# Gated linear attention with a gated feed-forward on one Trainium2 core: the first unit's two large products in full 32-bit type, weights split into parts behind them, and another order of the first transfers

## The chip, the cores and the metric

The kernel runs on one core of one Trainium2 chip. The metric is the device time of one execution in microseconds (us). A core has five engines with a queue each, worked off in order: TensorE (PE in the profile, its weight loads PEld), VectorE (DVE), ScalarE (ACT), GpSimd (POOL) and SyncE (SP), which here issues every transfer.

## The reference

For each of 4 batches and 8 heads a state of 48 x 48 runs over 768 positions; its output is the input of a feed-forward with a convolution of three taps as its gate.

```python
f = 1.0 / (1.0 + np.exp(-f_logit))
for t in range(S):
    state = f[:, :, t, :, None] * state + np.einsum('bhd,bhe->bhde', k[:, :, t], v[:, :, t])
    y[:, :, t] = np.einsum('bhd,bhde->bhe', q[:, :, t], state)
...
h = np.maximum(x @ w_in, 0.0)
for k in range(K):
    conv_out += conv_w[k][None, None, :] * hp[:, k:k + S, :]
gate = 1.0 / (1.0 + np.exp(-conv_out))
return (h * gate @ w_out).astype(np.float32)
```

x is y with its heads side by side (768 x 384 per batch), w_in is 384 x 1024, w_out 1024 x 384, and hp is h with a row of zeros on each side. The three weight tensors come as 64-bit floats.

## The kernel before

**Chunks.** The sequence is cut into chunks of 128 positions, six per batch, 24 in all, numbered n. For each chunk SyncE loads the gates' inputs (fb), k (kp), q (qp) and v. ScalarE takes exp and log of the gates (lines 167 and 168), TensorE sums them along the chunk with a triangular matrix (pl, line 193), and ScalarE raises the sums again (fi and fd, lines 197 and 198), by which k and q are multiplied (lines 210 and 211, on VectorE and GpSimd). TensorE transposes both (ptk, ptq, line 233) and ScalarE copies them out (kT, qT, line 235). Then come the scores (pa, line 281), VectorE's masked copy of them (am, line 283), the state's products and update (pk, lines 295 to 306) and the values (py, lines 318 and 321). For chunks 0 to 8 the cumulative sum is one product in full 32-bit type (tri32 and fb); later ones use two of type float32r, a reduced 32-bit type.

**Units.** Three chunks, half a batch, make a unit of the feed-forward, eight in all. The values are copied to xT twice: a high part in float32r by ScalarE (line 329) and what is left, the low part, by VectorE (line 330). Behind a unit's third chunk six transfers bring pieces of xT to other partitions (line 335). The first matrix product (mm1, line 358) makes eight blocks ph of 128 x 384; each takes three inner tiles, and for each of them three float32r products: high weight with high value, high weight with low value, low weight with high value. Behind each block come ScalarE's relu (hb, line 361) and first tap (line 363), VectorE's other taps (lines 369 and 370), ScalarE's tanh (line 372) and VectorE's closing multiplication (line 373); these are the gate steps, all in the tile g. The second product (mm2) goes by output tiles of 128 positions: g is split into high (gh, line 388, ScalarE) and low (gl, line 389, VectorE), and eight inner tiles with three float32r products each (line 395) make po, which ScalarE copies to ob and SyncE stores (lines 398 and 399). A unit with the first half of a batch owns two output tiles, the other one four.

**Weights.** Their 64-bit words are turned into two float32r parts by split_f64 (lines 90 to 107), piece by piece: w_in in six pieces of 128 x 512 (three inner tiles kt, two halves i of the 1024 columns), w_out in eight of 128 x 384. Per piece GpSimd clamps the upper words (line 98) and takes their sign (line 99), ScalarE scales the upper (line 100) and converts the lower words (line 101), VectorE merges them in two steps (lines 102 and 104), ScalarE casts the sum to the high part (line 106) and VectorE subtracts for the low one (line 107).

**What sets the order.** Everything is planned as small pieces with a number (lines 410 to 449), sorted by it, and written out; the numbers come from the table CFG and count in chunks. A scheduler then orders the instructions of each engine from there, so that the table moves them without fixing each place. From chunk 8 on the products of a chunk's values, state and scores are kept together (visit, lines 256 to 272). Raw weights, the tiles g and xT share slots: the raw halves of w_in and the first of w_out lie in the two slots of g, the other raw half of w_out in one of the three slots of xT.

## Time and profile before

| what | before |
|---|---|
| median of 3 runs (lowest to highest) | 373.13 us (373.02 to 373.95) |
| the profiled execution's own time | 373.25 us |
| its span, first to last instruction | 371.5 us |
| mean granted clock of TensorE | 0.97 of full speed |
| TensorE busy | 342.6 us, 92% |
| VectorE busy | 279.9 us, 75% |
| ScalarE busy | 239.4 us, 64% |
| GpSimd busy | 75.1 us, 20% |

Times in the profile run from the span's start; between its span and its own time lie 1.75 us. A row of the groups names line, engine, operation, output and inputs, shapes and count, then busy time, mean ns of one, and the idle time of the engine in front of it with what ended it. A row of a timeline names start, length, engine, line, operation and count, and in brackets the idle time in front of it. A full 32-bit product appears as two records. A row of stages names its bounds, its length, and for each engine busy time and count, then the granted clock, the DMA engines' busy share and GB/s. The chain of waits follows the work that ended last back to the start, with the time that each step adds to it.

### The profile page before, as it was taken

Reading aid. Unit: us, or ns where it says so; the run is one execution under the profiler, and the core shown is the slowest. Engines: PE = TensorE matmul, PEld = TensorE weight load, DVE = VectorE, ACT = ScalarE, POOL = GpSimd, SP = SyncE. Lnnn points to the kernel's source line nnn. Section 1 sums busy time; section 2 is a strip of 40 time slices with the busy share of each in tenths; the row PEclk is TensorE's granted clock in tenths of the full one; section 3 lists DMA queues with packets and bytes.
Section 4 is the critical chain, followed back from the end, with each engine's and each line's share of the span. In section 5 each row is a group of like instructions: output and inputs, shape, how many; then the busy total and the mean of one; then the engine's idle time right before and its main releaser. Section 6 shows DMA issues by size and latency. Waiting matters only on the chain.

```text
span 371.5 us, 7272 instructions
## 1 busy us (share of the span) xinstructions
PE 342.6 (92%) x2747; PEld 315.4 (85%) x2747; DVE 279.9 (75%) x407; ACT 239.4 (64%) x426; POOL 75.1 (20%) x103
## 2 busy tenths in 40 slices
...
GB/s 234 374 334 350 79 112 158 128 30 114 133 28 80 110 193 23 76 108 160 54 42 85 72 136 44 73 116 52 23 43 35 23 0 55 33 11 44 21 45 50
DMA packets 28853, 36.04 MB, mean 97 GB/s; under 512 B 10847, under 2 KB 20106, under 8 KB 28810
## 3 DMA queue, kind: packets, MB, share of 16 engines
...
## 4 chain that ended last, share of the span: by engine, by line
PE 59%; ACT 14%; DVE 11%; DMA 8%; issue 4%; SPq 1%; ACTq 0%; DVEq 0%
PE po L395 21%; PE ph L358 21%; PE py L321 5%; DMA wis<-in_moe_w_in_dram 4%; PE pa L281 4%; PE py L318 3%; DMA fb<-in_f_logit_dram 3%; DVE g L369 2%; PE pl L193 2%; DVE kp L210 2%; PE ptq L233 2%; ACT fb L167 2%; ACT g L363 1%; ACT fb L168 1%; DVE g L370 1%
## 5 line engine op out<-in xcount | busy, mean ns | idle before, releaser
L358 PE MATMUL ph<-xT,wi 128*128 128x384 f32 x576 | 112.6, 345 | 4.6 <-ACT ob L398 2.6
L358 PEld LDWEIGHTS ph<-xT,wi 128*128 128x128 f32 x576 | 101.1, 189 | 8.4 <-ACT ob L398 3.9
L395 PE MATMUL po<-wo,gh 128*128 128x384 f32 x384 | 99.4, 340 | 0.0
L395 PEld LDWEIGHTS po<-wo,gh 128*128 128x128 f32 x384 | 69.7, 188 | 0.1
L395 PE MATMUL po<-wo,gl 128*128 128x384 f32 x192 | 65.8, 343 | 0.0
L369 DVE SCALAR_TENSOR_TENSOR g<-hb,cw,g 128x384 f32<-128x384 f32 (+1 forms) x64 | 44.7, 701 | 14.6 <-ACT g L363 14.1
L372 ACT ACTIVATE g<-g 128x768 f32<-128x768 f32 (+1 forms) x32 | 27.1, 846 | 43.0 <-DVE g L370 42.9
L361 ACT ACTIVATE hb<-ph 128x384 f32<-128x384 f32 x64 | 31.2, 490 | 25.5 <-PE ph L358 25.4
L370 DVE SCALAR_TENSOR_TENSOR g<-hb,cw,g 128x384 f32<-128x384 f32 (+1 forms) x64 | 42.7, 666 | 3.4 <-DVE g L369 0.5
L373 DVE SCALAR_TENSOR_TENSOR g<-g,hb 128x768 f32<-128x768 f32 (+1 forms) x32 | 30.8, 964 | 16.7 <-ACT g L372 16.6
L389 DVE TENSOR_TENSOR gl<-g,gh 128x1024 fp32r<-128x1024 f32 (+4 forms) x34 | 32.1, 957 | 14.6 <-ACT gh L388 14.6
L363 ACT ACTIVATE g<-hb,cw 128x384 f32<-128x384 f32 (+1 forms) x64 | 39.3, 618 | 1.9
L211 POOL TENSOR_TENSOR qp<-qp,fd 128x384 f32<-128x384 f32 x22 | 28.8, 1307 | 53.3 <-ACT fd L198 43.3
L388 ACT CAST gh<-g 128x1024 fp32r<-128x1024 f32 (+4 forms) x34 | 26.4, 800 | 19.9 <-PE po L395 17.4
L395 PEld LDWEIGHTS po<-wo,gl 128*128 128x128 f32 x192 | 36.1, 188 | 0.9 <-issue 0.2
L321 PE MATMUL py<-am,v 128*48 128x128 f32 x384 | 28.9, 295 | 5.8 <-DVE am L283 5.8
L283 DVE COPY_PREDICATED am<-mask,pa 128x1024 f32<-128x1024 uint8 x24 | 31.6, 1316 | 1.8 <-PE pa L281 1.6
L281 PE MATMUL pa<-qT,kT 48*128 48x128 f32 x384 | 28.4, 285 | 3.5 <-ACT qT L235 3.5
L321 PEld LDWEIGHTS py<-am,v 128*48 128x48 f32 x384 | 21.9, 131 | 10.9 <-DVE am L283 6.8
L281 PEld LDWEIGHTS pa<-qT,kT 48*128 48x128 f32 x384 | 23.6, 187 | 8.2 <-ACT qT L235 4.9
L210 DVE TENSOR_TENSOR kp<-kp,fi 128x384 f32<-128x384 f32 x22 | 22.0, 1000 | 10.5 <-ACT fi L197 9.8
L318 PE MATMUL py<-qT,st 128*112 128x128 f32 x168 | 22.8, 279 | 0.0
...
## 6 DMA issues: line engine op xcount, KB each, us to landing
kp<-in_k_dram SPq DMA_DIRECT2D x24, 256.0 KB
qp<-in_q_dram SPq DMA_DIRECT2D x24, 256.0 KB
fb<-in_f_logit_dram SPq DMA_DIRECT2D x24, 192.0 KB
v<-in_v_dram SPq DMA_DIRECT2D x24, 192.0 KB
out_dram<-ob SPq DMA_DIRECT2D x24, 192.0 KB
wis<-in_moe_w_in_dram SPq DMA_DIRECT2D x6, 512.0 KB
...
```

What stands on the lines that cost most here:

```text
L281: nc.tensor.matmul(pa[:, j, p, :], kT[r, p, :], qT[r, p, :], start=True, stop=True)
L283: ready.setdefault(n, []).append(nc.vector.copy_predicated(am, mask, pa).ins)
L318: nc.tensor.matmul(py[:HP + D, p, :], s_b[n % 2][:, p, :], qT[:, p, :], start=(p == 0), stop=False)
L321: nc.tensor.matmul(py[HP * j:HP * j + D, p, :], vt[:, 2 * p + j, :], am[:, j, p, :], start=not inter and p == 0, stop=(p == NP - 1))
L358: nc.tensor.matmul(ph, wi[:, t, wl, f * P:(f + 1) * P], xts[b, hf][:, t, xl, :], start=(i == 0), stop=(i == 3 * KT - 1))
L361: nc.scalar.activation(hb[:, 2:HS + 2], ph, AF.Relu, scale=0.5)
L363: nc.scalar.activation(cv, hb[:, 1:n + 1], AF.Copy, scale=cw[:, 1, f:f + 1])
L369: nc.vector.scalar_tensor_tensor(cv, hb[:, 2:n + 2], cw[:, 2, f:f + 1], cv, ALU.mult, ALU.add)
L370: nc.vector.scalar_tensor_tensor(cv, hb[:, 0:n], cw[:, 0, f:f + 1], cv, ALU.mult, ALU.add)
L373: nc.vector.scalar_tensor_tensor(cv, cv, 1.0, h_b[:, fp:fp + 2, 1:n + 1], ALU.add, ALU.mult)
L389: nc.vector.tensor_tensor(lo, g[:, f:f + k], hi.bitcast(F32), ALU.subtract)
L395: nc.tensor.matmul(po, g[:, f, :], wo[:, f, wl, :], start=(i == 0), stop=(i == 3 * NF - 1))
```

## The change

**Types.** The function single replaces split_f64: it makes one 32-bit tile per weight piece out of the same words with the same two steps each on GpSimd, ScalarE and VectorE. The function split makes the high and low part out of that tile, with ScalarE's cast and VectorE's subtraction, and is planned by itself. For the first unit (u = 0, batch 0, first half) mm1 takes the 32-bit pieces and one product per inner tile, in full 32-bit type; so do the two output tiles that it owns, with g itself as the weight loaded, so that gh and gl are not made for them. The values of its three chunks are copied to xT once, in 32 bits, with no low part, and the transfers inside xT carry that half only. All other units compute as before.

**Tiles.** The high parts are wih and woh. The 32-bit pieces and the low parts share slots: seven for w_in's pieces, eight for w_out's. So a low part takes over the slot of an earlier 32-bit piece, once the first unit's products and the split have read it. The constant zeros for the products that keep TensorE warm at the start (wz) now lie in wih, where a high part is written later.

**Order.** In the table, the first nine chunks' gates are loaded 0.7 of a chunk earlier; w_in is loaded at -0.9 and 0.2 instead of -2.3 and -1.1 and converted from 2.6 and 3.3 on, instead of -0.7 and 0.9; w_out is loaded at 2.9 and 2.7 instead of 1.3 and 1.0 and converted from 4.0 on instead of 2.1; w_in is split from 4.6 and 6.0 on, w_out from 8.9 on; and the output tiles of each unit lie 0.9 instead of 1.2 thirds (or quarters) of a unit apart.

```diff
+    wl = ctx.enter_context(tc.tile_pool(name="wl", bufs=1))
...
     ft_all = const.tile([P, B, NC, NP], F32, name="ft_all")
-    wz = const.tile([P, WC], F32R, name="wz")
+    wih = const.tile([P, KT, DFF], F32R, name="wih")
+    woh = const.tile([P, NF, DM], F32R, name="woh")
+    wz = wih[:, KT - 1, DFF - WC:]
     nc.gpsimd.memset(wz.bitcast(F32), 0.0)
-    wi = const.tile([P, KT, 2, DFF], F32R, name="wi")
-    wo = const.tile([P, NF, 2, DM], F32R, name="wo")
+    w32, wlo = {}, {}
     cw = const.tile([P, 3, NF], F32, name="cw")
-    def split_f64(raw, n, hi, lo, nm):
+    def single(raw, n, w, nm):
         pr = raw.rearrange("p (n w) -> p n w", w=2)
         lw, hw = pr[:, :, 0], pr[:, :, 1]
...
         ms = wk.tile([P, 2, WC], I32, tag="gl", name=f"ms{nm}")
         m, s = ms[:r, 0, :n], ms[:r, 1, :n]
         hf, mf, sf = hw.bitcast(F32), m.bitcast(F32), s.bitcast(F32)
-        nc.gpsimd.tensor_scalar(hf, hf, F64_TOP, -F64_TOP, ALU.min, ALU.max)
-        nc.gpsimd.tensor_scalar(sf, hf, 0.0, 1.0, ALU.mult, ALU.mult)
-        nc.scalar.activation(mf, hf, AF.Copy, scale=2.0 ** -112)
+        nc.gpsimd.tensor_scalar(mf, hf, F64_TOP, -F64_TOP, ALU.min, ALU.max)
+        nc.gpsimd.tensor_scalar(sf, mf, 0.0, 1.0, ALU.mult, ALU.mult)
+        nc.scalar.activation(mf, mf, AF.Copy, scale=2.0 ** -112)
         nc.scalar.activation(lw, lw.bitcast(U32), AF.Copy, scale=2.0 ** -29)
         nc.vector.scalar_tensor_tensor(m, m, 3, s, ALU.logical_shift_left, ALU.bitwise_or)
-        w = hi.bitcast(I32) if lo is None else s
-        nc.vector.tensor_tensor(w, m, lw, ALU.add)
-        if lo is not None:
-            nc.scalar.copy(hi, mf)
-            nc.vector.tensor_tensor(lo, sf, hi.bitcast(F32), ALU.subtract)
+        nc.vector.tensor_tensor(w.bitcast(I32), m, lw, ALU.add)
+
+    def split(key, hi, name, **slot):
+        wlo[key] = wl.tile(list(hi.shape), F32R, name=name, **slot)
+        nc.scalar.copy(hi, w32[key])
+        nc.vector.tensor_tensor(wlo[key], w32[key], hi.bitcast(F32), ALU.subtract)
...
     def load_w_in(kt, i):
         nc.sync.dma_start(raw_in(kt, i), w_in[kt * P:(kt + 1) * P, i * WC:(i + 1) * WC].bitcast(I32))
+    def single_w_in(kt, i):
+        w32["i", kt, i] = wl.tile([P, WC], F32, tag="wi", name=f"wi{kt}_{i}", bufs=KT * DFF // WC + 1)
+        single(raw_in(kt, i), WC, w32["i", kt, i], f"wi{kt}_{i}")
+
     def split_w_in(kt, i):
-        cs = slice(i * WC, (i + 1) * WC)
-        split_f64(raw_in(kt, i), WC, wi[:, kt, 0, cs], wi[:, kt, 1, cs], f"wi{kt}_{i}")
+        split(("i", kt, i), wih[:, kt, i * WC:(i + 1) * WC], f"wil{kt}_{i}", tag="wi", bufs=KT * DFF // WC + 1)
     def load_w_out(f):
         nc.sync.dma_start(raw_out(f), w_out[f * P:(f + 1) * P, :].bitcast(I32))
+    def single_w_out(f):
+        w32["o", f] = wl.tile([P, DM], F32, tag="wo", name=f"wo{f}", bufs=NF)
+        single(raw_out(f), DM, w32["o", f], f"wo{f}")
+
     def split_w_out(f):
-        split_f64(raw_out(f), DM, wo[:, f, 0, :], wo[:, f, 1, :], f"wo{f}")
+        if f == 0:
+            split(("o", f), woh[:, f], f"wol{f}", tag="wi", bufs=KT * DFF // WC + 1)
+        else:
+            split(("o", f), woh[:, f], f"wol{f}", tag="wo", bufs=NF)
...
         xT = xts[b, hf]
         ts = slice((c % CPH) * P, (c % CPH + 1) * P)
         for r in [slice(0, HP + D)] if c > 0 or n == 0 else [slice(0, D), slice(HP, HP + D)]:
+            if (b, hf) == (0, 0):
+                nc.scalar.copy(xT[r, :, 0, ts].bitcast(F32), py[r])
+                continue
             nc.scalar.copy(xT[r, :, 0, ts], py[r])
             nc.vector.tensor_tensor(xT[r, :, 1, ts], py[r], xT[r, :, 0, ts].bitcast(F32), ALU.subtract)
         if c % CPH == CPH - 1:
             for t in range(KT):
                 for j in range(2):
                     s0, d0 = HP * j + GAP * t, HP * j + D
-                    nc.sync.dma_start(xT[d0:d0 + GAP, t, :, :].bitcast(F32), xT[s0:s0 + GAP, KT, :, :].bitcast(F32))
-
-    def moe(xts, wk, ps):
+                    m = 1 if (b, hf) == (0, 0) else 2
+                    nc.sync.dma_start(xT[d0:d0 + GAP, t, :m, :].bitcast(F32), xT[s0:s0 + GAP, KT, :m, :].bitcast(F32))
+
+    def moe(xts, wk, ps, whole):
         gts = {}
         def mm1(u, fp):
...
             for f in (fp, fp + 1):
                 hb = h_b[:, f]
                 ph = ps.tile([P, HS], F32, tag="mm", name=f"ph{u}_{f}", bufs=2)
-                i = 0
-                for t in range(KT):
-                    for wl, xl in ((0, 0), (0, 1), (1, 0)):
-                        nc.tensor.matmul(ph, wi[:, t, wl, f * P:(f + 1) * P], xts[b, hf][:, t, xl, :],
-                                         start=(i == 0), stop=(i == 3 * KT - 1))
-                        i += 1
+                fs = slice(f * P, (f + 1) * P)
+                i, cs = f * P // WC, slice(f * P % WC, f * P % WC + P)
+                if u < whole:
+                    for t in range(KT):
+                        nc.tensor.matmul(ph, w32["i", t, i][:, cs], xts[b, hf][:, t, 0, :].bitcast(F32),
+                                         start=(t == 0), stop=(t == KT - 1))
+                else:
+                    k = 0
+                    for t in range(KT):
+                        hi, lo = wih[:, t, fs], wlo["i", t, i][:, cs]
+                        for w, xl in ((hi, 0), (hi, 1), (lo, 0)):
+                            nc.tensor.matmul(ph, w, xts[b, hf][:, t, xl, :], start=(k == 0), stop=(k == 3 * KT - 1))
+                            k += 1
                 nc.scalar.activation(hb[:, 2:HS + 2], ph, AF.Relu, scale=0.5)
                 cv = gts[u][:, f, :n]
                 nc.scalar.activation(cv, hb[:, 1:n + 1], AF.Copy, scale=cw[:, 1, f:f + 1])
-                if u < CFG["tp"] and f % 2 < CFG["tf"]:
-                    t2 = wk.tile([P, WC], F32, tag="ob", name=f"t2{u}_{f}")[:, :n]
-                    nc.scalar.activation(t2, hb[:, 2:n + 2], AF.Copy, scale=cw[:, 2, f:f + 1])
-                    nc.gpsimd.tensor_tensor(cv, cv, t2, ALU.add)
-                else:
-                    nc.vector.scalar_tensor_tensor(cv, hb[:, 2:n + 2], cw[:, 2, f:f + 1], cv, ALU.mult, ALU.add)
+                nc.vector.scalar_tensor_tensor(cv, hb[:, 2:n + 2], cw[:, 2, f:f + 1], cv, ALU.mult, ALU.add)
                 nc.vector.scalar_tensor_tensor(cv, hb[:, 0:n], cw[:, 0, f:f + 1], cv, ALU.mult, ALU.add)
             cv = gts[u][:, fp:fp + 2, :n]
             nc.scalar.activation(cv, cv, AF.Tanh)
             nc.vector.scalar_tensor_tensor(cv, cv, 1.0, h_b[:, fp:fp + 2, 1:n + 1], ALU.add, ALU.mult)
         def mm2(b, m):
+            po = ps.tile([P, DM], F32, tag="mm", name=f"po{b}_{m}", bufs=2)
+            if b == 0 and m < whole * (CPH - 1):
+                for f in range(NF):
+                    nc.tensor.matmul(po, gts[0][:, f, m * P + 1:(m + 1) * P + 1], w32["o", f],
+                                     start=(f == 0), stop=(f == NF - 1))
+                return done(b, m, po)
             gh = wk.tile([P, NF, P], F32R, tag="gh", name=f"gh{b}_{m}")
             gl = wk.tile([P, NF, P], F32R, tag="gl", name=f"gl{b}_{m}")
             t0 = 0
...
                     nc.scalar.copy(hi, g[:, f:f + k])
                     nc.vector.tensor_tensor(lo, g[:, f:f + k], hi.bitcast(F32), ALU.subtract)
                 t0 += n
-            po = ps.tile([P, DM], F32, tag="mm", name=f"po{b}_{m}", bufs=2)
             i = 0
             for f in range(NF):
-                for g, wl in ((gh, 0), (gh, 1), (gl, 0)):
-                    nc.tensor.matmul(po, g[:, f, :], wo[:, f, wl, :], start=(i == 0), stop=(i == 3 * NF - 1))
+                hi, lo = woh[:, f], wlo["o", f]
+                for g, w in ((gh, hi), (gh, lo), (gl, hi)):
+                    nc.tensor.matmul(po, g[:, f, :], w, start=(i == 0), stop=(i == 3 * NF - 1))
                     i += 1
-            ob = wk.tile([P, WC], F32, tag="ob", name=f"ob{b}_{m}")[:, :DM]
+            done(b, m, po)
+
+        def done(b, m, po):
+            ob = wk.tile([P, DM], F32, tag="ob", name=f"ob{b}_{m}")
             nc.scalar.copy(ob, po)
             nc.sync.dma_start(out[b, m * P:(m + 1) * P, :], ob)
...
-    units = moe(xts, wk, ps)
+    units = moe(xts, wk, ps, 1)
...
     for i in range(DFF // WC):
         for kt in range(KT):
             plan(CFG["wil"][i] + 0.01 * kt, lambda kt=kt, i=i: load_w_in(kt, i))
-            plan(CFG["wis"][i] + 0.1 * kt, lambda kt=kt, i=i: split_w_in(kt, i))
+            plan(CFG["wis"][i] + 0.1 * kt, lambda kt=kt, i=i: single_w_in(kt, i))
+            plan(CFG["w2i"][i] + CFG["w2is"] * kt, lambda kt=kt, i=i: split_w_in(kt, i))
     plan(CFG["cw"], load_cw)
     plan(-CFG["a"] + 0.01, lambda: warm(12))
     for f in range(NF):
         plan(CFG["wol"][f // 4] + 0.01 * f, lambda f=f: load_w_out(f))
-        plan(CFG["wos"] + f * CFG["wo"], lambda f=f: split_w_out(f))
+        plan(CFG["wos"] + f * CFG["wo"], lambda f=f: single_w_out(f))
+        plan(CFG["w2o"] + CFG["w2os"] * f, lambda f=f: split_w_out(f))
     for u in range(2 * B):
         w1, w2 = units(u)
         for i, w in enumerate(w1):
```

SyncE's first transfers, before (k, q and gates of chunk 0, the first half of w_in in three pieces, and so on):

```order
L181 DMA kp0_84<-in_k_dram 128x512
L181 DMA qp0_88<-in_q_dram 128x512
L158 DMA fb0_113<-in_f_logit_dram 128x384
L124 DMA wis0_117<-in_moe_w_in_dram 128x1024 x3
L186 DMA v0_121<-in_v_dram 128x384
L181 DMA kp1_85<-in_k_dram 128x512
L181 DMA qp1_89<-in_q_dram 128x512
L158 DMA fb0_113<-in_f_logit_dram 128x384
```

and now:

```order
L171 DMA fb0_113<-in_f_logit_dram 128x384
L194 DMA kp0_87<-in_k_dram 128x512
L194 DMA qp0_91<-in_q_dram 128x512
L171 DMA fb0_113<-in_f_logit_dram 128x384
L199 DMA v0_120<-in_v_dram 128x384
L194 DMA kp1_88<-in_k_dram 128x512
L194 DMA qp1_92<-in_q_dram 128x512
L171 DMA fb0_113<-in_f_logit_dram 128x384
L199 DMA v1_158<-in_v_dram 128x384
L194 DMA kp2_89<-in_k_dram 128x512
L194 DMA qp2_93<-in_q_dram 128x512
L127 DMA wis0_162<-in_moe_w_in_dram 128x1024 x3
```

The three pieces of w_in have moved behind the gates, k and q of chunks 0 to 2; the gates of chunk 0 stand first.

ScalarE at chunk 0, before, from its two raised sums (fi0, fd0) to the copy of its transposed k (kT0):

```order
L197 ACTIVATE fi0_128<-pl0_125 128x384
L198 ACTIVATE fd0_127<-pl0_125 128x384
L106 CAST wi_105<-mswi0_0_199 128x512
L167 ACTIVATE fb0_113<-fb0_113 128x384
L206 COPY ft_all_101<-pl0_125 48x4 x2
L168 ACTIVATE fb0_113<-fb0_113 128x384
L100 ACTIVATE mswi2_0_220<-wis0_117 128x512
L106 CAST wi_105<-mswi1_0_211 128x512
L235 COPY kT0_172<-ptk0_167 128x512
```

and now, one row further, to its transposed q (qT0):

```order
L210 ACTIVATE fi0_127<-pl0_124 128x384
L211 ACTIVATE fd0_126<-pl0_124 128x384
L103 ACTIVATE wis0_162<-wis0_162 128x512
L219 COPY ft_all_104<-pl0_124 48x4 x2
L103 ACTIVATE wis0_162<-wis0_162 128x512
L248 COPY kT0_171<-ptk0_166 128x512
L248 COPY qT0_178<-ptq0_173 128x512
```

The scalings (mswi), casts (wi) and gate steps have left this place, the gate steps to ahead of fi0; two conversions of the lower words of w_in (wis) stand ahead of kT0, and each waits for its transfer.

VectorE at the first unit's first gate steps (g0), before, with the last low parts of w_out (wo) ahead of them:

```order
L104 ISA mswo7_794<-wos1_338,mswo7_794 128x768
L107 TENSOR_TENSOR wo_106<-mswo6_728,wo_106 128x384
L330 TENSOR_TENSOR xT0_1_624<-py3_611,xT0_1_624 112x4x128
L107 TENSOR_TENSOR wo_106<-mswo7_794,wo_106 128x384
L283 COPY_PREDICATED am0_91<-mask1_82,pa4_687 128x1024
L369 SCALAR_TENSOR_TENSOR g0_636<-hb_99,cw_107,g0_636 128x384
L305 TENSOR_TENSOR stmp4_0_746<-pk4_737,st0_95 48x192
L369 SCALAR_TENSOR_TENSOR g0_636<-hb_99,cw_107,g0_636 128x384
L370 SCALAR_TENSOR_TENSOR g0_636<-hb_99,cw_107,g0_636 128x384
L306 TENSOR_TENSOR st1_96<-stmp4_0_746,ft_all_101 48x4x48
```

and now:

```order
L105 ISA wo0_625<-wos0_490,mswo0_626 128x768
L319 TENSOR_TENSOR st1_99<-stmp4_1_664,ft_all_104 48x4x48
L388 SCALAR_TENSOR_TENSOR g0_584<-hb_102,cw_109,g0_584 128x384 x2
L110 TENSOR_TENSOR wil1_0_734<-wi1_0_465,wih_106 128x512
L389 SCALAR_TENSOR_TENSOR g0_584<-hb_102,cw_109,g0_584 128x384 x2
L104 SCALAR_TENSOR_TENSOR mswo1_692<-mswo1_692 128x384
L110 TENSOR_TENSOR wil2_0_766<-wi2_0_482,wih_106 128x512
L105 ISA wo1_691<-wos0_490,mswo1_692 128x768
L110 TENSOR_TENSOR wil0_1_881<-wi0_1_542,wih_106 128x512
L104 SCALAR_TENSOR_TENSOR mswo2_721<-mswo2_721 128x384
```

Between the gate steps stand low parts of w_in (wil) and the merges of w_out (mswo, and the unnamed kind behind it that writes wo), which stood ahead of them before.

8 lines of the change are left out of this document (4 added, 4 removed).

## The prediction

> **What bounds the kernel now.** I read the page's busy shares first, then the busy time by stage, then the timeline of each engine at the start, and last the groups by line. All sums below are made against the profiled execution, 373.25 us with a span of 371.5 us; the median of the runs, 373.13 us, lies 0.12 us below it. The stages, each row with its bounds, its length and then busy time and count of TensorE (PE), its weight loads, VectorE (DVE), ScalarE (ACT) and GpSimd (POOL), the granted clock, the DMA share and GB/s:
>
> ```profile
> span 371.5 us, 7272 instructions
> 10.00:40.00 30.00, 18.60 (x208) 13.34 (x207) 27.29 (x39) 26.58 (x61) 22.10 (x27) 0.89 0.94 338
> 63.40:126.30 62.90, 57.73 (x476) 51.30 (x475) 50.28 (x77) 49.97 (x81) 10.22 (x13) 0.95 0.34 92
> 126.30:345.00 218.70, 215.59 (x1725) 207.86 (x1724) 171.03 (x242) 135.08 (x231) 31.77 (x38) 1.00 0.24 66
> 345.00:371.50 26.50, 20.82 (x118) 20.50 (x117) 7.48 (x10) 7.50 (x14) 0.00 (x0) 0.96 0.12 41
> ```
>
> The reader sees two kernels. From 126.3 us on TensorE is busy for 215.59 of 218.70 us: whatever reaches that point sooner ends sooner by as much, as long as TensorE gets no more work behind it. From 10 to 40 us TensorE is busy for only 18.60 of 30 us, and VectorE (27.29) and ScalarE (26.58) are nearly full, with the chunks' work and with the conversion of the weights. So the end moves by what the beginning gains, less what is added to TensorE. Five moments mark the beginning: ScalarE's copy of chunk 2's values into xT, SyncE's transfers inside xT, the first product of the first unit, VectorE's first gate multiplication, and the cumulative sum of chunk 11, which stands at almost the same place of TensorE's order in both programs:
>
> ```profile
> 46.73 0.58 ACT L329 CAST xT<-py 112x512 fp32r<-112x512 f32 x1 [0.67 <-PE py L321]
> ...
> 49.80 4.28 SPq L335 DMA_DIRECT2D xT<-xT  x6
> ...
> 53.79 2.36 PE L358 MATMUL ph<-xT,wi 128*128 128x384 f32 x12 [1.26 <-DMA xT<-xT]
> ...
> 63.44 0.60 DVE L369 SCALAR_TENSOR_TENSOR g<-hb,cw,g 128x384 f32<-128x384 f32 x1
> ...
> 126.32 0.34 PE L193 MATMUL pl<-cgh,tri 128*128 128x384 f32 x1
> ```
>
> **Part 1: the first product starts earlier.** The copy at 46.73 stands in ScalarE's queue behind weight steps. Their prices, w_in and w_out apart:
>
> ```profile
> L100 ACT ACTIVATE mswo<-wos 128x384 f32<-128x384 f32 x8 | 4.5, 558 | 2.2 <-DVE wo L107 1.4 <-DVE c L104 0.8
> L101 ACT ACTIVATE wos<-wos 128x384 int32<-128x384 uint32 x8 | 4.4, 559 | 0.0
> L106 ACT CAST wo<-mswo 128x384 fp32r<-128x384 f32 x8 | 4.1, 514 | 2.2 <-DVE mswo L102 2.1
> L100 ACT ACTIVATE mswi<-wis 128x512 f32<-128x512 f32 x6 | 4.0, 668 | 0.2 <-DVE wi L107 0.2
> L106 ACT CAST wi<-mswi 128x512 fp32r<-128x512 f32 x6 | 3.7, 614 | 0.6 <-DVE mswi L102 0.6
> ...
> 48.89 0.49 ACT L197 ACTIVATE fi<-pl 128x384 f32<-128x384 f32 x1 [0.53 <-PE pl L193]
> 49.27 0.49 ACT L198 ACTIVATE fd<-pl 128x384 f32<-128x384 f32 x1
> ```
>
> Ahead of the copy stand, by the two orders, 5 casts of w_in fewer (6 to 1), 3 scalings of w_in (6 to 3), 3 casts and 3 scalings of w_out (all), and 4 conversions of w_out's low words (8 to 4): 5 x 0.614 + 3 x 0.668 + 3 x 0.514 + 3 x 0.558 + 4 x 0.559 = 10.5 us. The last two rows show that a step begins 0.1 us before the one ahead has ended (0.38 us from start to start at 0.49 us each), so 18 steps give 8.7 us.
>
> Against it stands a new wait. In the changed order ScalarE's conversion of the first w_in piece stands ahead of chunk 0's kT copy, and that piece now comes behind three chunks of gates, q and k:
>
> ```profile
> 11.55 0.65 ACT L101 ACTIVATE wis<-wis 128x512 int32<-128x512 uint32 x1 [0.79 <-DMA wis<-in_moe_w_in_dram]
> ...
> kp<-in_k_dram SPq DMA_DIRECT2D x24, 256.0 KB
> fb<-in_f_logit_dram SPq DMA_DIRECT2D x24, 192.0 KB
> wis<-in_moe_w_in_dram SPq DMA_DIRECT2D x6, 512.0 KB
> ```
>
> Before, k, q, the gates and three w_in pieces (2 x 256 + 192 + 3 x 512 = 2240 KB) had landed at 11.55. Now three of gates, two of v (as large), six of k and q and one piece (5 x 192 + 6 x 256 + 512 = 3008 KB) must land, 768 KB more; at the 338 GB/s of the 10 to 40 us row that is 2.3 us, so 13.9 us. The two scalings that ScalarE did there before are gone, 1.3 us. I estimate 1.3 us of net wait: the copy comes at 46.73 - 8.7 + 1.3 = 39.3 us, 7.4 us sooner.
>
> From the copy to the product it took 7.06 us: the copy itself, VectorE's subtraction of the low part (gone for this unit), and until 49.80 a wait of SyncE's queue for a free k buffer ahead of the transfers. The transfers then needed 3.99 us to the product. The k buffer is freed by chunk 3's state products, which TensorE reaches by about the same 39.3 us; I count 0.6 us for the copy and 3.99, so the product starts at 43.9 us, **9.9 us sooner**. The transfers are half as large now, for which I count nothing.
>
> **Part 2: the products themselves get dearer.** Three f32r products become one in full 32 bits, 24 times in the first matrix and 16 times in the second:
>
> ```profile
> 141.65 4.24 PE po L395 x24
> ...
> 136.89 0.87 PE py L318 x8
> ...
> 66.75 0.81 PE L193 MATMUL pl<-fb,tri 128*128 128x384 f32 x2
> ...
> L318 PE MATMUL py<-qT,st 128*112 128x128 f32 x168 | 22.8, 279 | 0.0
> ```
>
> 24 f32r products of 384 columns take 4.24 us in the chain, 0.177 each, 0.53 for three. For the f32 kind there are two rows: four products of 128 columns (eight records) take 0.87 us in a stream, 0.2175 each, so 0.65 us at three times the columns; and one product of exactly this shape, the cumulative sum, takes 0.81 us from its first start to its last end, standing alone. In a stream the ends overlap, so I take 0.65: 40 x (0.65 - 0.53) = **4.8 us more**, all on the path because TensorE is the bound behind. The ends are 40 x (0.65 - 0.53) and 40 x (0.81 - 0.53) = 11.2 us. The Trainium skill, page "FP8 and Floating Point Precision", section TensorE Precision Notes, speaks against the change: true FP32 takes four passes through the array, where three replace it now. By that rule a product would cost a third more than it does, by the stream's row a bit under a quarter; what the first would make of the time is a rival below.
>
> **Part 3: conversion moves behind the first product.** VectorE's prices:
>
> ```profile
> L104 DVE CUSTOM_DVE_ANT_0 mswo<-wos,mswo 128x768 uint16<-128x768 uint16 x8 | 5.5, 683 | 0.1
> L102 DVE SCALAR_TENSOR_TENSOR mswo<-mswo 128x384 int32<-128x384 int32 x8 | 4.4, 548 | 0.0
> L107 DVE TENSOR_TENSOR wi<-mswi,wi 128x512 fp32r<-128x512 f32 x6 | 4.8, 797 | 0.6 <-ACT wi L106 0.2
> L107 DVE TENSOR_TENSOR wo<-mswo,wo 128x384 fp32r<-128x384 f32 x8 | 4.7, 592 | 0.3
> L389 DVE TENSOR_TENSOR gl<-g,gh 128x1024 fp32r<-128x1024 f32 x20 | 24.4, 1222 | 11.8 <-ACT gh L388 11.7
> ```
>
> In the old order no weight step stands behind VectorE's first gate multiplication. In the new one 7 merges of w_out (0.548 + 0.683 each), 5 low parts of w_in and 8 of w_out do; two subtractions of the first unit's g fall away: 7 x 1.231 + 5 x 0.797 + 8 x 0.592 - 2 x 1.222 = 14.9 us more. Seven of the low parts of w_out are wanted only by the third output tile, beyond the cumulative sum of chunk 11, so 10.8 us press. The first gate multiplication came 9.65 us after the first product; six f32 products precede it, 0.7 us more, so it comes at 43.9 + 9.65 + 0.7 = 54.2 us. VectorE then has 50.28 + 10.8 = 61.1 us to do. At 0.93 of its time (a little over the 27.29 of 30 us that it reached from 10 to 40 us) this ends at 54.2 + 65.7 = 119.9 us. TensorE, with the waits it has now, comes there at 126.3 - 9.9 + 4.8 = 121.2 us. So TensorE still binds, by 1.3 us, and the cover for VectorE's moved work is its present idle time, 62.9 - 50.28 = 12.6 us. Low parts also wait in VectorE's queue for slots that TensorE's products must have read, with gate multiplications behind them; no row shows such a wait, it is bounded by nothing and by that margin's whole loss. I count **1.0 us**. ScalarE gains less there (8 scalings, one cast of w_in and 7 of w_out, less two casts of g) and has 12.9 us idle in the same stretch.
>
> The output tiles' spacing in the plan changes for all units (0.9 for 1.2 of a third). From 126.3 us on this only reorders TensorE's products, and TensorE is idle for 3.1 us of 218.7 there: nothing counted, 1 us either way.
>
> **Sum**: -9.9 + 4.8 + 1.0 = -4.1 us: 373.25 - 4.1 = **369.1 us**, likeliest range of its own 367.0 to 371.5 (2.3 us dearer products above, one more microsecond of start and no slot waits below).
>
> **The rivals.** *Slower: GpSimd holds VectorE.* GpSimd's clamp and sign steps of w_out move too, from beside the merges to beside the gate multiplications:
>
> ```profile
> 67.77 2.60 DVE L369 SCALAR_TENSOR_TENSOR g<-hb,cw,g 128x384 f32<-128x384 f32 x1 [0.75 <-ACT g L363]
> ...
> 67.30 2.65 POOL L173 TENSOR_TENSOR cgl<-fb,cgh 128x1152 fp32r<-128x1152 f32 x1 [7.06 <-ACT cgh L172]
> ...
> L98 POOL TENSOR_SCALAR wos<-wos 128x384 f32<-128x384 f32 x8 | 6.8, 857 | 0.8 <-DMA wos<-in_moe_w_out_dram 0.5
> L99 POOL TENSOR_SCALAR mswo<-wos 128x384 f32<-128x384 f32 x8 | 5.2, 654 | 8.4 <-DVE wo L107 8.2
> ```
>
> A multiplication of 0.60 us took 2.60 while GpSimd's 2.65 us subtraction ran. The 16 steps of w_out are 12.0 us. If VectorE loses h of them, it reaches the point at 54.2 + (61.1 + h) / 0.93; that passes the present 126.3 from h = 6.0 us on. With h = 9 it is 129.6: +3.3, 376.5 us. For it speaks the row; against it, that the means of the merges already hold such delays from the busy GpSimd before. Chance 0.19. *Slower: the f32 product costs its lone 0.81.* 11.2 instead of 4.8 gives +2.3, 375.6 us; against it stands the stream of 0.2175. Chance 0.08. *Less gain: a product costs four of the present passes.* 4 x 0.177 = 0.707 us, 7.1 us more in all instead of 4.8: 371.4 us. For it speaks that these products have 384 columns and new weights each time, against it the 0.65. Chance 0.10. *No gain: ScalarE stands still for its transfers.* Six conversions of w_in stand among the first chunks' copies in its queue, each behind a transfer of its own. Should they cost 4.1 us more than I counted, the start gains 5.8 and the time is 373.2 us. Chance 0.12. *Faster: the waits of the middle go too.* TensorE idles for 62.9 - 57.73 = 5.2 us between 63.4 and 126.3, at a clock of 0.95. If these go, and VectorE works 0.98 of the time, the point is reached at 54.2 + 62.3 = 116.5 us: -9.8, 363.4 us. Against it, VectorE and ScalarE get fuller there, not emptier. Chance 0.15.
>
> **How the numbers follow.** The forecast has 0.36. Differences within 0.3%, 1.1 us, are about what a measurement of this kernel cannot tell from none. Faster by more: the forecast, the dearer passes, the fast rival and a sliver of the standstill, 0.62. Slower: the two slow rivals less their edge near zero, 0.26. The same: 0.12. The range runs from 363, a little below the fast rival, to 377, half a microsecond above the likelier slow one; what it leaves out is VectorE losing all 12 us and a start that gains more than counted.
>
> **What would show it.** Right: first product at 43 to 45 us, TensorE's first-unit group of 24 products (48 records) at about 0.65 us each, chunk 11's cumulative sum at 121 to 123 us, and the stretch behind it as long as now. Wrong: a first product later than 48 us with ScalarE waiting for w_in transfers; f32 products spaced by 0.8 us; or TensorE idle for more than 8 us between the first gate multiplication and chunk 11, released by VectorE.

## The result, and the profile after

The kernel after took 371.02 us (median of 20 runs), the kernel before beside it on the same chip 374.0 (median of 20): a ratio of 0.9904, 95% interval 0.9877 to 0.9932, so faster by 0.96%. The medians are over all runs, the ratios leave disturbed runs out (four of the 20 of the kernel after; without them its median is 370.3). The profiled execution after took 370.4 us, with a span of 368.6 for 371.5 before. The same four stages as in the prediction, with the same columns:

```profile
span 368.6 us, 7146 instructions
10.00:40.00 30.00, 26.50 (x329) 20.64 (x329) 18.81 (x31) 25.19 (x60) 13.10 (x16) 0.89 0.89 307
63.40:126.30 62.90, 56.57 (x401) 44.29 (x401) 58.24 (x92) 46.84 (x82) 20.04 (x23) 0.92 0.32 84
126.30:345.00 218.70, 214.37 (x1718) 206.27 (x1717) 171.41 (x243) 134.22 (x230) 31.91 (x37) 1.00 0.23 63
345.00:371.50 26.50, 17.99 (x103) 17.67 (x101) 4.81 (x6) 6.32 (x10) 0.00 (x0) 0.94 0.11 40
```

From 10 to 40 us TensorE is now busy for 26.50 us instead of 18.60, VectorE for 18.81 instead of 27.29. From 63.4 to 126.3 it is VectorE that is nearly full, 58.24 of 62.90 us (50.28 before), and TensorE's granted clock is 0.92 (0.95). Behind that little changed. The five moments of the prediction, from the engines' timelines: chunk 2's copy, the transfers inside xT, the first product, the first gate multiplication, chunk 11's cumulative sum:

```profile
36.36 0.58 ACT L343 COPY xT<-py 112x512 f32<-112x512 f32 x1
...
37.02 3.75 SPq L352 DMA_DIRECT2D xT<-xT  x6
...
40.57 2.75 PE L376 MATMUL ph<-xT,wi 128*128 128x384 f32 x8
...
56.12 1.62 DVE L388 SCALAR_TENSOR_TENSOR g<-hb,cw,g 128x384 f32<-128x384 f32 x2
...
122.73 0.42 PE L206 MATMUL pl<-cgh,tri 128*128 128x384 f32 x1
```

The first product comes 13.2 us sooner (53.79 before), chunk 11 only 3.6 us sooner (126.32), the end 2.9. Where the 9.6 us between went, two rows of stages say, from the first product to chunk 11, before and then after:

```profile
53.79:126.32 72.53, 67.36 (x557) 59.32 (x558) 59.46 (x91) 56.35 (x93) 12.64 (x16) 0.95 0.35 96
```

```profile
40.57:122.73 82.16, 74.77 (x523) 54.57 (x521) 72.81 (x112) 62.76 (x110) 30.15 (x33) 0.94 0.37 105
```

TensorE is busy for 7.4 us more there and idle for 2.2 us more. Part of the busy time is not more work but a slower clock, and that hangs on the waits. The longest ones of the middle stand in TensorE's timeline after, in brackets:

```profile
66.58 0.81 PE L246 MATMUL ptk<-ident,kp 128*128 128x128 f32 x4 [2.88 <-DVE kp L223]
...
82.48 1.65 PE L206 MATMUL pl<-fb,tri 128*128 128x384 f32 x2 [2.52 <-ACT kT L248]
```

And these are the windows of 2 us around them (bounds, length, then busy time and count of each engine, the granted clock third from the end):

```profile
66.00:68.00 2.00, 1.42 (x6) 1.11 (x7) 2.00 (x5) 0.97 (x3) 0.77 (x2) 0.74 0.00 0
68.00:70.00 2.00, 2.00 (x5) 1.08 (x4) 2.00 (x3) 1.97 (x5) 2.00 (x3) 0.50 0.00 0
...
80.00:82.00 2.00, 0.00 (x0) 0.00 (x0) 2.00 (x3) 1.97 (x6) 1.92 (x4) 0.65 0.54 88
82.00:84.00 2.00, 1.52 (x2) 0.50 (x2) 2.00 (x4) 1.34 (x3) 0.63 (x1) 0.50 0.51 183
84.00:86.00 2.00, 2.00 (x29) 1.93 (x30) 1.94 (x4) 0.87 (x2) 0.89 (x1) 0.50 0.30 54
86.00:88.00 2.00, 2.00 (x21) 1.57 (x17) 1.97 (x5) 0.58 (x1) 0.11 (x1) 0.64 0.45 85
88.00:90.00 2.00, 2.00 (x12) 1.59 (x11) 2.00 (x5) 1.13 (x2) 0.53 (x1) 1.00 0.54 173
```

Behind each of the two waits TensorE is busy without a gap, but at half its clock. So a span can be split into three: TensorE's work, its idle time (length less busy time, window by window) and what it loses at the halved clock (busy time x (1 - granted clock): 1.00 us in the row from 84 to 86). Summed over the windows of a span, of this kernel, the one before and the experiments below:

| profile | idle to 40 us | 40 to 130 | behind 130 | lost at halved clock to 40 | 40 to 130 | span | median (all runs) and ratio to before, 95% |
|---|---|---|---|---|---|---|---|
| before | 13.4 | 6.7 | 8.8 | 2.9 | 6.0 | 371.5 | 374.0 |
| after | 6.4 | 7.4 | 9.9 | 2.8 | 4.0 | 368.6 | 371.0, 0.9904 (0.9877 to 0.9932) |
| e1 order alone | 8.5 | 10.4 | 9.7 | 6.4 | 3.1 | 370.1 | 372.3, 0.9944 (0.9913 to 0.9974) |
| e2 types alone | 11.0 | 6.9 | 9.9 | 4.6 | 7.9 | 378.3 | 379.0, 1.0097 (1.0057 to 1.0136) |
| e3 tiles' spacing | 6.4 | 7.4 | 9.7 | 0.0 | 4.4 | 366.8 | 370.9, 0.9903 (0.9862 to 0.9943) |
| e4 group 4 in 32 bits | 5.9 | 11.2 | 10.8 | 6.2 | 1.3 | 374.7 | 376.0, 1.0004 (0.9960 to 1.0047) |
| e5 gates' transfers | 8.4 | 10.2 | 9.5 | 2.6 | 2.2 | 369.0 | 369.7, 0.9872 (0.9835 to 0.9908) |
| e6 one subtraction moved | 6.1 | 7.9 | 9.7 | 0.0 | 4.4 | 366.4 | 367.6, 0.9822 (0.9782 to 0.9861) |
| e7 24 products in f32r | 5.8 | 12.7 | 8.5 | 3.1 | 6.6 | 370.5 | 371.9, 0.9927 (0.9890 to 0.9963) |
| e8 warm-up | 6.7 | 8.2 | 9.0 | 0.0 | 5.3 | 369.1 | 371.8, 0.9941 (0.9908 to 0.9975) |
| e9 no low parts | 6.0 | 7.0 | 9.4 | 0.0 | 1.5 | 365.5 | 369.6, 0.9876 (0.9823 to 0.9929) |
| e10 casts on VectorE | 6.1 | 8.5 | 8.5 | 2.9 | 4.1 | 367.2 | 368.3, 0.9837 (0.9792 to 0.9882) |
| e11 five subtractions moved | 6.0 | 8.3 | 11.5 | 4.6 | 3.0 | 370.8 | 371.0, 0.9904 (0.9868 to 0.9940) |
| e12 e5 and e6 | 8.1 | 8.1 | 10.3 | 2.5 | 9.1 | 373.9 | 374.8, 0.9985 (0.9945 to 1.0025) |

The runs of e1 to e4, of e5 to e8 and of e9 to e12 were made on three chips, each beside the kernel before, so the ratios are what to compare. Each row's split is of one execution; that of e9 is the fastest of its six.

What a span has beyond these five columns is work: 333.7 us before, 338.1 after. That remainder is not exact: the kernels with the same products as after range from 335.7 (e12) to 341.6 (e9). A likely reason, not shown, is that at half the clock not all of TensorE's time doubles, so that the loss is an upper bound. After against before, the split reads: 7.0 us of idle time gone at the start, 0.7 and 1.1 us more idle behind it, 2.1 us less lost at the halved clock, and some 4.4 us more work, known to a few us only: -2.9 in all.

The same split in windows of 1 us, cut at the two moments instead of at 40 and 130 us, says where the 13.2 us came from and went. Ahead of the first product TensorE runs the same chunk work in both kernels (351 and 352 records), with 8.5 us less idle time (14.9 before, 6.4 after) and 3.6 us less lost at the halved clock. From there to chunk 11 the idle time is 2.2 us more, the loss 1.6 us more and the work 5.9 us more.

### The profile page after: what moved, and what is told of

Same layout as the page of the kernel before. It is cut to its first block, busy times and chain, and to the rows that moved or that the text cites. A ratio compares the mean times of both kernels' runs of the same rounds, so it can differ in the third digit from the quotient of the medians.

```text
span 368.6 us, 7146 instructions
## 1 busy us (share of the span) xinstructions
PE 344.8 (94%) x2707; PEld 306.9 (83%) x2707; DVE 274.7 (75%) x402; ACT 236.4 (64%) x424; POOL 77.6 (21%) x103
## 4 chain that ended last, share of the span: by engine, by line
PE 72%; ACT 10%; DMA 6%; DVE 5%; SPq 3%; issue 2%; POOL 0%; ACTq 0%; DVEq 0%
PE po L420 24%; PE ph L383 22%; PE pa L294 6%; PE py L334 5%; PE py L331 4%; DMA wos<-in_moe_w_out_dram 3%; PE po L398 2%; PE ph L376 2%; PE pl L206 2%; DMA wis<-in_moe_w_in_dram 2%; PE ptq L246 2%; DVE g L388 2%; PE ptk L246 2%; PE pk L308 1%; DMA fb<-in_f_logit_dram 1%
## 5 line engine op out<-in xcount | busy, mean ns | idle before, releaser
L383 PE MATMUL ph<-xT,wih 128*128 128x384 f32 x336 | 88.5, 344 | 0.8 <-ACT ob L426 0.8
L383 PEld LDWEIGHTS ph<-xT,wih 128*128 128x128 f32 x336 | 59.8, 188 | 3.7 <-ACT ob L426 1.7
L420 PE MATMUL po<-woh,gh 128*128 128x384 f32 x176 | 59.5, 338 | 0.7 <-ACT hb L385 0.7
L420 PE MATMUL po<-woh,gl 128*128 128x384 f32 x176 | 60.0, 341 | 0.0
L420 PE MATMUL po<-wol,gh 128*128 128x384 f32 x176 | 59.5, 338 | 0.0
L383 PE MATMUL ph<-xT,wil 128*128 128x384 f32 x168 | 56.9, 339 | 0.0
L388 DVE SCALAR_TENSOR_TENSOR g<-hb,cw,g 128x384 f32<-128x384 f32 (+1 forms) x64 | 46.0, 724 | 14.2 <-ACT g L387 13.7
L224 POOL TENSOR_TENSOR qp<-qp,fd 128x384 f32<-128x384 f32 x22 | 28.0, 1273 | 65.7 <-ACT fd L211 55.1
L420 PEld LDWEIGHTS po<-woh,gl 128*128 128x128 f32 x176 | 33.0, 188 | 1.2 <-issue 0.2
L420 PEld LDWEIGHTS po<-woh,gh 128*128 128x128 f32 x176 | 33.0, 188 | 1.0 <-ACT hb L385 1.0
L420 PEld LDWEIGHTS po<-wol,gh 128*128 128x128 f32 x176 | 33.0, 187 | 0.0
L223 DVE TENSOR_TENSOR kp<-kp,fi 128x384 f32<-128x384 f32 x22 | 23.2, 1055 | 12.5 <-ACT fi L210 12.4
L383 PEld LDWEIGHTS ph<-xT,wil 128*128 128x128 f32 x168 | 31.5, 188 | 0.1
```

The source lines that it names most:

```text
L224: (nc.vector if CFG["eq"] == "d" or n < CFG["q0"] else nc.gpsimd).tensor_tensor(qp[:, :, :D], qp[:, :, :D], fd, ALU.mult)
L383: nc.tensor.matmul(ph, w, xts[b, hf][:, t, xl, :], start=(k == 0), stop=(k == 3 * KT - 1))
L388: nc.vector.scalar_tensor_tensor(cv, hb[:, 2:n + 2], cw[:, 2, f:f + 1], cv, ALU.mult, ALU.add)
L420: nc.tensor.matmul(po, g[:, f, :], w, start=(i == 0), stop=(i == 3 * NF - 1))
```

## The experiments

Theory at the outset: the start's gain, less the dearer products, less what VectorE's full queue takes back in the middle. Rivals: the gain is the transfers' order alone; the tiles' spacing has a part; GpSimd's hold on VectorE decides the middle.

**e1, the order alone**, in the kernel before:

```diff
-f1=2.6, wil=(-2.3, -1.1), wis=(-0.7, 0.9), wol=(1.3, 1.0), wos=2.1
+f1=3.3, wil=(-0.9, 0.2), wis=(2.6, 3.3), wol=(2.9, 2.7), wos=4.0
```

> The kernel before with the new table's places for the gates' transfers, the weights' transfers and the weights' conversion (gates 3.3 chunks ahead, w_in and w_out loaded and converted late), and nothing else: three f32r products everywhere, low parts made with the conversion, ahead of the first unit. Theory: the start is gained by taking weight steps out of ScalarE's queue ahead of chunk 2's copy, and most of that comes with the order alone. Ahead of the copy stand 3 casts, 2 scalings and 2 low-word conversions more than in the kernel after, some 4 us, so the copy comes at about 40 us (36.4 after, 46.7 before), the first product, with VectorE's subtraction still in the way, at 44 to 47 us (40.6 after, 53.8 before). No dearer products, so the time lies at or below the kernel after's: 368 to 371 us against 374.0 before. Rival: without the full 32-bit type the low parts hold the first product, at 51 us or later, and the time is that of before within 1.5 us.

Copy and product, from the timelines of e1:

```profile
41.97 0.58 ACT L329 CAST xT<-py 112x512 fp32r<-112x512 f32 x1
...
49.55 2.37 PE L358 MATMUL ph<-xT,wi 128*128 128x384 f32 x12
```

The copy comes 4.8 us sooner than before, 2 us short of the 40 us expected, the product falls between the two expectations, and so does the time: 0.56% below before. Idle time to 40 us falls by 4.9 us. So the order alone brings more than half of the gain of 0.96%; that the rest is there at all is not clear of noise, since the intervals of e1 and of the kernel after overlap (0.9913 to 0.9932).

**e2, the types alone**, in the kernel after:

```diff
-f1=3.3, wil=(-0.9, 0.2), wis=(2.6, 3.3), wol=(2.9, 2.7), wos=4.0
+f1=2.6, wil=(-2.3, -1.1), wis=(-0.7, 0.9), wol=(1.3, 1.0), wos=2.1
```

> The kernel after with the table of before for the gates' transfers, the weights' transfers and the first conversion, and nothing else changed: first unit in full 32-bit products, split into parts behind them, weights first. Theory: the type alone takes 3 to 4 casts and the subtraction of chunk 2 out of the way, so the first product comes at 47 to 50 us (53.8 before, 40.6 after); this gain of 4 to 7 us is paid back by 4.8 us of dearer products: 372 to 375 us, the time of before within 1.5 us. Rival: the type is what gains, the order nothing: first product by 44 us and the time of the kernel after within 1.1 us.

The first product came at 49.87 us, as the theory had it, yet the kernel is 0.97% slower than before, not level with it. Idle time to 40 us falls by 2.4 us only, which does not pay for the dearer products (4.3 us or more, see below), and more is lost at the halved clock (12.5 us for 8.9). By idle time to 40 us the two halves of the change nearly add up: 4.9 and 2.4 us alone, 7.0 together. The types without the order lose.

**e3, the tiles' spacing**, in the kernel after:

```diff
-m2s=0.9
+m2s=1.2
```

> The kernel after with the output tiles' spacing in the plan back at 1.2. Theory: TensorE is busy for 214.4 of 218.7 us behind chunk 11, so this only reorders its products: the time of the kernel after within 1.1 us. Rival: the closer tiles bring part of the gain, by filling TensorE's waits between the units: 1.1 to 3 us slower than the kernel after.

0.9903 against 0.9904: the spacing does nothing that these runs can see (the interval is 0.4% wide to each side), as predicted.

**e4, the fourth group's gates in one product**, in the kernel after:

```diff
-lf=3
+lf=4
```

> The kernel after with the fourth group's gates (chunks 9 to 11) in one full 32-bit product instead of two f32r parts: GpSimd's 2.82 us subtraction at 59.08 us and ScalarE's 1.19 us cast go, three cumulative sums take 0.81 instead of 0.35 us twice overlapped, some 0.3 us more each, 0.9 in all. Theory: in the middle VectorE's queue is what loses part of the start's gain, and its merge of 2.98 us at 59.33 (0.55 by itself) is held by that GpSimd operation: VectorE gains 2.4 us, TensorE's wait of 2.88 us at 66.58 shrinks by 1 to 2.4 us, chunk 11's cumulative sum comes 0 to 1.5 us sooner, the time is 0 to 1.5 us below the kernel after. Rival: VectorE's delay is made good by idle time before chunk 11, and only the dearer sums count: 0.9 us slower.

Neither: 1.0004 for 0.9904. TensorE's waits of the middle grew from 7.4 to 11.2 us; TensorE's order moved too, from behind the fifth block of the first matrix on, so this run does not price the hold.

**e5, the gates' transfers back**, in the kernel after:

```diff
-f1=3.3
+f1=2.6
```

> The kernel after with the gates' transfers back at 2.6 chunks ahead instead of 3.3, nothing else. Theory: the start is gained by what stands ahead of chunk 2's copy in ScalarE's queue, and the gates' place is a small part of it: first product at 40 to 43 us, time 0 to 1.5 us above the kernel after. Rival: it is the order of the transfers at the very start that pays: first product 3 us or more later, time 2 to 4 us above the kernel after.

Rather faster than the kernel after (0.9872, the intervals overlap), although the first product comes at 44.27 us. The gates' place is not what pays, and the moment of the first product is by itself no measure of the time: in e5 more of chunk 3's work stands ahead of it, and chunk 11 comes only 1.2 us later (123.94). Nor is idle time by itself: e5 has 2.0 us more of it up to 40 us and 2.8 us more from there to 130 us.

**e6, one subtraction from GpSimd to VectorE**, in the kernel after:

```diff
-gv=2
+gv=4
```

> The kernel after with the low part of the fourth group's gates subtracted by VectorE instead of GpSimd. It takes GpSimd's 2.82 us operation at 59.08 us away and gives VectorE some 1.2 us of its own. Theory: VectorE's merge of 2.98 us at 59.33 was held for the length of GpSimd's operation (0.55 us by itself), and the wait of 2.88 us of TensorE at 66.58, with the halved clock behind it, hangs on that: the merge takes 0.6 us, the wait shrinks by 1 us or more, chunk 11's cumulative sum comes 1 to 3 us sooner and the time is 1 to 3 us below the kernel after. Rival: VectorE's queue is full there whichever way, other steps take the place: the time of the kernel after within 1.1 us, or above it.

First the two timelines of the kernel after, VectorE's merge and GpSimd's subtraction, then VectorE's of e6:

```profile
59.33 2.98 DVE L104 SCALAR_TENSOR_TENSOR mswo<-mswo 128x384 int32<-128x384 int32 x1
...
59.08 2.82 POOL L186 TENSOR_TENSOR cgl<-fb,cgh 128x1152 fp32r<-128x1152 f32 x1 [1.74 <-ACT cgh L185]
```

```profile
58.98 0.55 DVE L104 SCALAR_TENSOR_TENSOR mswo<-mswo 128x384 int32<-128x384 int32 x1
59.45 0.68 DVE L110 TENSOR_TENSOR wil<-wi,wih 128x512 fp32r<-128x512 f32 x1
60.05 0.55 DVE L105 CUSTOM_DVE_ANT_0 wo<-wos,mswo 128x768 uint16<-128x768 uint16 x1
60.52 1.35 DVE L186 TENSOR_TENSOR cgl<-fb,cgh 128x1152 fp32r<-128x1152 f32 x1
```

The hold is real: the merge takes 0.55 us without GpSimd beside it, 2.98 with. This is the fastest kernel measured, 367.6 us, and its interval lies below that of the kernel after. But the profile does not show the gain where the theory put it. The wait of 2.88 us became 1.67, but the one ahead of it on the same step grew from 0.91 to 1.95, and the one behind it from 2.52 to 3.97. The first of the three in the kernel after, then all three in e6:

```profile
49.89 0.63 PE L246 MATMUL ptk<-ident,kp 128*128 128x128 f32 x4 [0.91 <-DVE kp L223]
```

```profile
49.61 0.63 PE L246 MATMUL ptk<-ident,kp 128*128 128x128 f32 x4 [1.95 <-DVE kp L223]
...
65.08 0.66 PE L246 MATMUL ptk<-ident,kp 128*128 128x128 f32 x4 [1.67 <-DVE kp L223]
...
80.85 1.65 PE L206 MATMUL pl<-fb,tri 128*128 128x384 f32 x2 [3.97 <-ACT kT L248]
```

From the first product (38.99) to chunk 11 (121.15) it is 82.16 us in e6, and 82.16 in the kernel after; the profile of e6 ends sooner because nothing was lost at a halved clock up to 40 us, which e3 with the old subtraction had too.

**e7, the first matrix's products of the first unit in f32r, with a constant in the place of w_in**, in the kernel after:

```diff
-                        nc.tensor.matmul(ph, w32["i", t, i][:, cs], xts[b, hf][:, t, 0, :].bitcast(F32),
-                                         start=(t == 0), stop=(t == KT - 1))
+                        for j in range(3):
+                            nc.tensor.matmul(ph, tri, xts[b, hf][:, t, 0, :], start=(t + j == 0), stop=(t == KT - 1 and j == 2))
...
-                nc.scalar.copy(xT[r, :, 0, ts].bitcast(F32), py[r])
+                nc.scalar.copy(xT[r, :, 0, ts], py[r])
```

> The kernel after with the first unit's 24 full 32-bit products of the first matrix each replaced by three f32r products of the same size, all with the triangular constant as weights, so that the first unit leaves out the first weight matrix and no low parts are needed; the transfers, the conversions and the second matrix's 16 full 32-bit products stay. Theory: the products' price is paid in full: 24 x (0.65 - 0.53) = 2.9 us, so 2 to 4 us below the kernel after. Rival: four passes of 0.177 us each, 4.2 us. Second rival: VectorE's queue sets chunk 11, and what TensorE saves becomes idle time: within 1.1 us of the kernel after.

The second rival. The cheaper products bring nothing (0.9927 for 0.9904): idle time from 40 to 130 us grows from 7.4 to 12.7 us. The wait on VectorE's kp step, from TensorE's timeline of e7:

```profile
65.63 1.09 PE L246 MATMUL ptk<-ident,kp 128*128 128x128 f32 x4 [4.69 <-DVE kp L223]
```

What TensorE saves there it waits for, 4.69 us instead of 2.88. Its products also need no piece of w_in, and other instructions moved, so this is a strong sign rather than a proof.

**e8, more warm-up products**, in the kernel after:

```diff
     plan(-CFG["a"] + 0.01, lambda: warm(12))
+    plan(-0.79, lambda: warm(3))
+    plan(0.01, lambda: warm(3))
```

> The kernel after with six more warm-up products of 512 columns behind chunk 0's cumulative sum, whose results nobody reads. In the traces of three kernels with nearly the same program up to there, the granted clock is 0.50 for 0, 6 and 13 us between 12 and 27 us, and the first product of the first unit comes at 39.06, 40.57 and 43.48 us. Theory: TensorE is idle for a third of the time from 9 to 16 us, which halves its clock in some runs, and since the weight steps are gone from ScalarE's queue a slow TensorE now delays the first product: filled, the clock stays at 1.0, the first product comes at 39 to 40.5 us and the median is 1 to 2.5 us below the kernel after, with less spread. Rival: six products of 0.2 to 0.4 us stand ahead of chunk 0's work and delay it, and the clock is halved all the same: 0.5 to 2 us slower.

The clock did stay at 1.0 up to 40 us in the profile, and nothing was gained: the first product came at 40.51 us, 1.5 us later than in the unfilled kernels whose clock stayed up, and the time is 0.9941 of before (0.9904 for the kernel after, intervals overlapping). This filler is no cure.

**e9 and e10, relief for one queue each**, in the kernel after; both leave out the low parts of the weights, and the products that took one take the high part once more. e9 first, then e10:

```diff
-        wlo[key] = wl.tile(list(hi.shape), F32R, name=name, **slot)
+        wlo[key] = hi
         nc.scalar.copy(hi, w32[key])
-        nc.vector.tensor_tensor(wlo[key], w32[key], hi.bitcast(F32), ALU.subtract)
```

```diff
-        wlo[key] = wl.tile(list(hi.shape), F32R, name=name, **slot)
-        nc.scalar.copy(hi, w32[key])
-        nc.vector.tensor_tensor(wlo[key], w32[key], hi.bitcast(F32), ALU.subtract)
+        wlo[key] = hi
+        nc.vector.tensor_copy(hi, w32[key])
```

> The kernel after without the low parts of both weight matrices: VectorE's 14 subtractions behind the first unit (6 x 0.82 + 8 x 0.56 = 9.4 us) are left out, and the products that took a low part take the high part once more, so TensorE's work is the same in number and size. Theory: VectorE's queue is what makes TensorE wait in the middle (7.4 us idle and 4.0 us lost at halved clock between 40 and 130 us in the kernel after): both together shrink by 3 us or more, the time is 3 to 6 us below the kernel after. Rival: ScalarE's queue does it (from 69 to 83 us it runs almost without a gap, three table loads of 1.28 us among its steps, and the wait of 2.52 us at 82.48 is for its kT copy): less than 1.1 us of difference.

> The same without low parts, and with the 14 casts that make the high parts moved from ScalarE to VectorE: VectorE has about what it has in the kernel after (14 casts for 14 subtractions), ScalarE 6 x 0.64 + 8 x 0.51 = 7.9 us less. Theory (VectorE's queue sets the middle): the time of the kernel after within 1.1 us, and 2 us or more above the run without low parts. Rival (ScalarE's queue): 3 to 6 us below the kernel after. If both engines' queues count, both runs are 1 to 3 us below it.

9.4 us off VectorE give 0.9876, 7.9 us off ScalarE 0.9837; the kernel after has 0.9904. By these ratios the runs are about 1.0 and 2.5 us below it, so neither queue alone is worth the 3 us of the theory or the rival. It looks like the third case, both count, but e9's interval contains the ratio of the kernel after, and e10's still touches the interval of that kernel. In the profiles idle time from 40 to 130 us is 7.0 and 8.5 us (7.4), the loss at the halved clock 1.5 and 4.1 us (4.0). In e9 the two together fall by 2.9 us, in its fastest run; in e10 they do not fall at all. Which of the queues sets the middle stays open.

**e11 and e12, all five subtractions moved, and e5 with e6**, in the kernel after; e11 first:

```diff
-gv=2
+gv=8
```

```diff
-f1=3.3, gv=2
+f1=2.6, gv=4
```

> The kernel after with the low part of all five later groups' gates subtracted by VectorE, not the fourth group's alone. Theory: behind chunk 11 TensorE is idle for only 4 us of 219, two waits of 1.6 and 0.4 us on VectorE among them, so what the other four groups' holds cost is at most 2 us: 0 to 2 us below the run with the fourth group alone (367.6 us), which was 2 to 3 us below the kernel after. Rival: the four subtractions of 1.35 us on VectorE delay the gate multiplications that TensorE waits for: 0.5 to 2 us above that run.

> The kernel after with the fourth group's subtraction on VectorE and the gates' transfers back at 2.6 chunks ahead. The one alone gave 367.6, the other 369.4 us (370.3 for the kernel after). Theory: they act at different places (the middle, and the idle time and clock of the start) and add up: 366 to 367.5 us. Rival: the second was luck with the clock: 367.5 to 370 us.

Both went against the theory, and further than the rival had it: 0.9904 and 0.9985. The two edits that were each at or below the kernel after give, together, the time of before. In the profile of e12 one wait of 3.30 us at 75.92 is followed by the longest halved stretch of the study, with a second wait of 2.01 us at 85.22 inside it. The windows of e12 show the last part:

```profile
86.00:88.00 2.00, 2.00 (x20) 1.63 (x17) 2.00 (x5) 1.30 (x3) 0.66 (x2) 0.50 0.42 89
88.00:90.00 2.00, 2.00 (x10) 1.78 (x9) 1.94 (x5) 1.74 (x3) 0.01 (x1) 0.50 0.46 126
90.00:92.00 2.00, 2.00 (x10) 1.38 (x8) 1.97 (x4) 0.86 (x1) 0.00 (x0) 0.50 0.38 98
92.00:94.00 2.00, 2.00 (x8) 1.96 (x8) 1.71 (x2) 1.98 (x3) 0.00 (x0) 0.50 0.00 0
94.00:96.00 2.00, 2.00 (x8) 1.91 (x7) 0.00 (x0) 1.51 (x3) 0.00 (x0) 0.50 0.00 0
96.00:98.00 2.00, 2.00 (x12) 1.90 (x12) 0.36 (x1) 1.53 (x5) 0.00 (x0) 0.68 0.00 0
```

TensorE is busy throughout at a clock of 0.50; 9.1 us are lost from 40 to 130 us. e11 holds the same edit as e6 and four more, and is 0.9904 for 0.9822. Each of these edits also moves some of the instructions behind it in the order, and with them the places at which TensorE waits. So what e6's gain is made of stays open, and its six runs are few; it is the fastest version measured, and its interval lies below that of the kernel after.

## Why the prediction was right, and which of its steps were not

The sign and the size were right: faster, 370.4 us profiled and 371.0 at the median for a forecast of 369.1, within the forecast's own 367.0 to 371.5. That it came so near is partly luck: the start gained 3.3 us more than its term, the middle cost 2.8 us more than its term, and the two errors nearly cancel.

**Part 1** was too small. The copy came at 36.36 for 39.3 us predicted: the counted queue steps are gone, but no net wait for w_in came in their place (the first conversion stood at 11.85 us, not 13.9). From copy to product it took 4.21 us for the 4.6 counted. So the first product was 13.2 us sooner, for 9.9: 8.5 us of TensorE's idle time and 3.6 us at the halved clock, which the step had not counted, make up most of it. The step took this moment for time gained. That held between these two kernels, where the same chunk work stands ahead of it; it need not hold, as e5 shows with a first product 3.7 us later and no slower kernel.

**Part 2** had the price right, 0.65 us. Two groups of the first matrix and one output tile in TensorE's timeline after, each with the row that follows it (two records a product):

```profile
51.83 4.04 PE L376 MATMUL ph<-xT,wi 128*128 128x384 f32 x12
55.70 0.38 PE L331 MATMUL py<-qT,st 128*112 128x128 f32 x2
...
58.31 2.20 PE L376 MATMUL ph<-xT,wi 128*128 128x384 f32 x6
60.44 0.71 PE L294 MATMUL pa<-qT,kT 48*128 48x128 f32 x8
...
99.94 5.43 PE L398 MATMUL po<-wo,g 128*128 128x384 f32 x16
104.91 0.81 PE L383 MATMUL ph<-xT,wih 128*128 128x384 f32 x2
```

From start to start it is 3.87 us for six products, 2.13 for three and 4.97 for eight: 0.65, 0.71 and 0.62 each. With 24 at 0.65 to 0.71 and 16 at 0.62, for 0.53 before, the change adds 4.3 to 5.8 us. The stretch to chunk 11 has 5.9 us more work, of which one inner tile's 0.5 us stood behind chunk 11 before, so it agrees. Neither rival on this price came in full. The Trainium skill, page "FP8 and Floating Point Precision", section TensorE Precision Notes, counts four passes for a true 32-bit product; four of the 0.177 us would be 0.71, an estimate by that rule, which the group of three reaches and the longer streams stay below. What did not hold up is "all on the path because TensorE is the bound behind": e7 took the 24 dearer products out again and gained nothing, since TensorE then waited longer from 40 to 130 us.

**Part 3** foresaw the full VectorE, and with 62.13 of the 66.61 us from its first gate multiplication to chunk 11 busy, 0.93, even its share. Chunk 11 came at 122.73 us for 122.2 (121.2 and the 1.0 for slot waits). But two errors met there: a start too small by 3.3 us, and a first gate multiplication 15.5 us behind the first product for the 10.4 counted. ScalarE's first step on the first unit's result, at 50.86 us, stood behind conversions of w_out, of which two waited for their transfers. From ScalarE's timeline after:

```profile
44.76 0.56 ACT L103 ACTIVATE wos<-wos 128x384 int32<-128x384 uint32 x1 [0.98 <-DMA wos<-in_moe_w_out_dram]
...
48.22 0.55 ACT L103 ACTIVATE wos<-wos 128x384 int32<-128x384 uint32 x1 [1.47 <-DMA wos<-in_moe_w_out_dram]
...
50.86 0.49 ACT L385 ACTIVATE hb<-ph 128x384 f32<-128x384 f32 x1
```

That is the rival "ScalarE stands still for its transfers", one matrix later than it was put, and with 2.45 us; what the late step cost in the end no run measured. The step that failed is "TensorE still binds, by 1.3 us", with 1.0 us for waits. It carried over TensorE's present idle time and added the 1.0; in the event TensorE was idle 2.2 us longer on the way to chunk 11 and lost 1.6 us more at the halved clock, a loss the step put at nothing: 3.8 us. The step's own sum shows why: with the start as measured it has TensorE at 126.3 - 13.2 + 4.8 = 117.9 us and VectorE at 56.12 + 65.7 = 121.8, so the order of the two turned round. That VectorE's queue alone set the place is not shown; e9 speaks against it.

**Part 4**, the spacing: nothing, as predicted (e3).

**The slow rival**, GpSimd's hold on VectorE, exists (2.98 us for 0.55, e6), but its one long case is a gate subtraction, of a kind that held VectorE in the kernel before too, and not the 12 us of w_out's steps it counted; it stays far below the 6.0 us from which it would have decided. **The fast rival**, that the waits of the middle go, is refuted by the 7.4 us (6.7 before).
